# Windowed attention, Fourier mixing and an MLP on one core: new landing times in the planner, a later start for the last batch's loads, and a split last output tile

## The chip, the cores and the metric

One core of a Trainium2 chip. The metric is the device time of one execution in microseconds (us), median of several runs. The kernel before has 281.84 us, the median of five runs (280.18, 281.34, 281.84, 282.03, 282.28).

The engines of the core work side by side, each through its own queue in order: PE (TensorE, matmuls, with the weight loads PEld beside it), DVE (VectorE), ACT (ScalarE), POOL (GpSimd), SP (SyncE, which here only issues transfers). A transfer is issued by an engine's queue and lands later; semaphores tell other engines when.

## The reference

Four batches of 768 rows, 8 heads of 64, so rows of 512. First attention, in which a row sees the 96 rows up to itself and the first 8 rows, with a bias that falls with the distance:

```python
scores = scale * q @ k.T + bias
scores = np.where(is_global | is_local, scores, -1e9)
x = softmax(scores) @ v
```

Then the heads are put side by side, and per batch:

```python
mixed = np.real(np.fft.fft(np.fft.fft(x, axis=1), axis=2))
u = x + mixed
un = (u - mean(u)) / np.sqrt(var(u) + 1e-06)
out = u + np.maximum(un @ w_ch1, 0.0) @ w_ch2
```

with w_ch1 of 512 x 2048 and w_ch2 of 2048 x 512. Inputs and output are fp32; the matmuls work in fp16.

## The kernel before

**Names.** b is the batch (0 to 3). Within a batch, attention goes by pairs of heads, hp 0 to 3; n = 4b + hp counts pairs over all batches, so q7 and k7 are the q and k of batch 1's last pair, and q12 to q15 belong to batch 3. The MLP goes by chunks of 256 rows, three to a batch: c = 3b + pr, 0 to 11, each with two row tiles t of 128.

**Attention.** `load` (L353) issues q, k (384 KB each) and v (two transfers of 192 KB) of a pair on SP into staging buffers of tag qs (3) and vs (2). `cast_qk` (L400) makes fp16 of q and k, from batch 1 on by an ACT activation of about 0.8 us or on POOL; v is cast on POOL. `trans` (L489) transposes q and k on PE (tile pt, 12 matmuls at L498) and DVE or ACT evacuates it to qkT. `score` (L519) has three groups g for a pair: PE makes sc, ACT takes the exponential into er (L566; numbered so that er_10 is that of pair 5's second group), DVE multiplies it by the bias mask into ex. `v_global` and `glob` (pvg, pgl) do the eight global rows; `av` (L646, tile pav) makes the result, which DVE divides into x.

**Fourier mixing.** `bounce` (L701) writes x to DRAM in two halves and reads it back in another order of rows as xr, in two transfers (L719); from batch 1 on ACT issues all of this. DVE folds x by sums and differences (tags zy, eA, ww), PE multiplies by cosine and sine tables (`y_unit`, tile py), DVE or ACT evacuates it (zy, L896 and L898), `mirror` (L911) copies four pieces in reverse order on ACT or POOL (L929), and `u_unit` (L952) makes tile pu on PE (16 matmuls, L963), to which DVE adds xr, with the row sums (u, L984). un is the centred u (L1004, L1006); `nt_unit` (L1025) transposes it (ptu, evacuated to unT); squares on ACT (L1013) and two small POOL operations (L1020, L1021) give rstd.

**MLP.** `ph_unit` (L1056): 8 matmuls of 128 x 256 into a bank ph, then a relu into hT on ACT (L1072) or DVE (L1073). `pg_unit` (L1079): a row tile of 128 x 512 in four quarters of 4 matmuls each (L1089); after the last quarter DVE adds rstd * pg + u into ob (L1100) and the tile is stored as 256 KB (L1105), from ACT for c under 6, from SP after. The banks ph and pg are two each, the banks xx, for all else, two. w1 and w2 come in quarters of 512 KB, issued by POOL (L1177, L1180).

**What sets the order.** All instructions are written out by a planner (`Plan`, L18). It keeps a clock for each engine and for the transfers, and for each result a time at which it is expected (`tok`). `run` chooses the PE group that can start first out of four streams: MIX (Fourier mixing), ATT (attention, both with a look ahead of ten), PH and PG (in order); `emit` puts the work that follows a PE group on the engine that would finish it first. The instructions of an engine run in the order in which the planner wrote them, whether its times come true or not; an instruction that waits holds up all behind it on its engine.

For the loads of batches 1 and 2 the planner doesn't compute when they land but takes it from a table, `LAND` (L343), by n and (q, k, v), through `landed` (L346):

```python
pl.tok[key] = max(pl.t["SP"] + 3.0, LAND[n][w])
```

So the table decides where casts of q and k stand on ACT and POOL, when the planner believes a pair can be transposed, what it puts on PE before that, and, through the buffers that come free, in which order SP issues the loads. A load of batch 1 is not written before the bounce of batch 0 has been issued. For batch 2 there is a gate on the chip (L358): `hold` (L1188) issues on SP a transfer of 32 elements from a piece of w2 to DRAM, and that waits until this piece of w2 has been loaded; everything that stands behind it on SP waits with it. Batch 3's loads have no such gate: they are issued when a staging buffer is free.

Of the kernel before, what the change touches and what calls it, by code (L numbers as in the profile page):

```python
# [10 lines left out]
FP32 = mybir.dt.float32  # L11
AF = mybir.ActivationFunctionType
ALU = mybir.AluOpType
# [4 lines left out]
class Plan:  # L18
# [96 lines left out]
    def run(self, streams):  # L115

        left = [list(s) for s, _ in streams]
        while True:
            best = None
            for i, s in enumerate(left):  # L120
                for k, (needs, ring, _) in enumerate(s[:self.LOOK if streams[i][1] else 1]):
                    if not self.known(needs):
                        continue
                    r = self.at(needs, "PE")
                    if ring is not None:

                        there = [(self.rings[g][0], g) for g in ring if self.rings[g]]
                        if not there:
                            continue
                        t, g = min(there)  # L130
                        r = max(r, t + self.SEM)
                    else:
                        g = None
                    c = (max(r, self.t["PE"]), i, k, g or "")
                    if best is None or c < best:
                        best = c
            op = self.first()
            if op is not None and (best is None or op[0] <= best[0]):
                self.emit(op[4])
            elif best is not None:  # L140
                if self.fill is not None and best[0] - self.t["PE"] > 0.6:
                    self.fill(best[0])
                needs, ring, fn = left[best[1]].pop(best[2])
                if ring is not None:
                    self.slot(best[3])
                fn(best[0], best[3])
                self.promote()
            elif not any(left) and not self.pending:
                return
            else:  # L150
                raise RuntimeError("stuck: " + str([[n for n in s[0][0] if n not in self.tok] for s in left if s])
                                   + str([[n for n in p[2] if n not in self.tok] for p in self.pending][:5]))


def mm_us(n, k=1):
    return k * max(n / 2400.0 + 0.0025, 0.029)
# [6 lines left out]
def dve(n):  # L163
    return 0.15 + n / 960.0
# [11 lines left out]
def kernel(  # L176
# [105 lines left out]
    def free(tag, i):  # L282
        i -= NBUF[tag]
        return [("free", tag, i)] if i >= 0 else []

    def buf(tag, i, shape, dtype, users):
        pl.users(("free", tag, i), users)
        return wk.tile(shape, dtype, tag=tag, name=f"{tag}_{i}", bufs=NBUF[tag])
# [24 lines left out]
    def fill(until):  # L313
# [15 lines left out]
        for i in range(n):  # L329
# [10 lines left out]
    TT = {}  # L340


    LAND = {4: (43.5, 43.3, 47.3), 5: (51.6, 55.5, 54.0), 6: (57.4, 60.9, 59.2), 7: (65.9, 67.0, 64.9),  # L343
            8: (79.4, 81.6, 84.8), 9: (86.6, 91.0, 88.2), 10: (92.8, 96.3, 94.8), 11: (100.0, 102.5, 98.4)}

    def landed(n, w):  # L346
        def then(t):
# [5 lines left out]
    def load(b, hp, which):  # L353
        n = HP * b + hp
        h0 = 2 * hp
        vtag, vi = ("u", hp) if b == 0 else ("vs", n - HP)
        stage[("vs", n)] = (vtag, vi)
        gate = [("hold", b)] if b == 2 else [("xri", 0)] if b == 1 else []  # L358
        if which == "v" and b == 0:
            def run():  # L360
                t = buf(vtag, vi, [P, 2 * NS, Dh], FP32, 1)
                stage[("v", n)] = t
                qk_dma(t.rearrange("p (j t) d -> p j (t d)", t=2), v, b, h0)
            pl.later([("SP", 0.45, run)], free(vtag, vi), 0.0, [("ld", "v", n)], dma=1.34)
        elif which == "v":
            def run():
                t = buf(vtag, vi, [P, 2 * NS, Dh], FP32, 1)
                stage[("v", n)] = t
                src = v[b, h0:h0 + 2].rearrange("h s d -> (h s) d").rearrange("(n m t) d -> t m n d", m=64, t=2)
                for t2 in range(2):  # L370
                    nc.sync.dma_start(t[64 * t2:64 * t2 + 64], src[t2])
            pl.later([("SP", 0.9, run)], free(vtag, vi) + gate, 0.0, [("ld", "v", n)], lat=(0.0, 4.0, 6.0, 5.0)[b], dma=2.45, then=landed(n, 2))
        elif b == 0 and hp < 3:
            cell = {}

            def run(cell=cell):
                cell[0] = buf("hT", hp, [P, 2, NS, 2 * Dh], FP32, 2)
                for w, src in enumerate((q, k)):
                    qk_dma(cell[0][:, w], src, b, h0)
            pl.later([("SP", 0.9, run)], free("hT", hp), 0.0, [("ld", "qk", n, w) for w in range(2)], dma=2.68,  # L380
                     then=lambda t: pl.tok.__setitem__(("ld", "qk", n, 0), t - 1.34))
            for w in range(2):
                cast_qk(b, hp, w, lambda w=w, cell=cell: cell[0][:, w], ("hT", hp))
        else:
            for w, src in enumerate((q, k)):
                cell = {}
                i = 2 * (n - 3) + w

                def run(cell=cell, src=src, i=i):
                    cell[0] = buf("qs", i, [P, NS, 2 * Dh], FP32, 1)  # L390
                    qk_dma(cell[0], src, b, h0)
                pl.later([("SP", 0.45, run)], free("qs", i) + gate, 0.0, [("ld", "qk", n, w)],
                         lat=(0.0, 4.0, 6.0, 5.0)[b], dma=1.34, then=landed(n, w))
                cast_qk(b, hp, w, lambda cell=cell: cell[0], ("qs", i))
# [684 lines left out]
    def pg_unit(c, t, part):  # L1079
# [26 lines left out]
            pl.later([("ACT" if c < 6 else "SP", 0.45, st)], [("ob", i)], 0.0, [], [("free", "ob", i)], lat=1.6, dma=0.7)  # L1106
        PG.append((needs, ("pg",) if part == 0 else None, run))


    def dma_const(dst, src, us, tok, needs=()):  # L1110
        pl.later([("SP", 0.45, lambda: nc.sync.dma_start(dst, src.ap()))], needs, 0.0, [tok], lat=0.2, dma=us)

    with tc.manual_schedule():
# [74 lines left out]
        def hold(n, src):  # L1188

            nc.sync.dma_start(dr.tile([1, 32], FP16, tag=f"hold{n}", name=f"hold{n}", bufs=1), src)  # L1190
        pl.later([("SP", 0.5, lambda: hold(2, w2[0:1, 4, 0:32]))], [("w2", 1)], 0.0, [("hold", 2)])
        for b in range(B):
            if b:
                for hp in range(HP):
                    load(b, hp, "qk")
                    load(b, hp, "v")
                    cast_v(b, hp)
            if b == 0:
                for hp in range(HP):
                    trans(b, hp)  # L1200
                    for g in range(3):
                        score(b, hp, g)
                    if hp:
                        v_place(hp - 1)
                v_global(b, (0,))
                glob(b, (0,))
                for jp in range(NP):
                    av(b, (0, 1), jp)
                v_place(3)
                v_global(b, (1,))  # L1210
                glob(b, (1,))
                for jp in range(NP):
                    av(b, (2,), jp)
                for jp in range(NP):
                    av(b, (3,), jp)
            else:
                trans(b, 0)
                trans(b, 1)
                for hp in range(HP):
                    for g in range(3):  # L1220
                        score(b, hp, g)
                    if hp + 2 < HP:
                        trans(b, hp + 2)
                    if hp == 2:
                        v_global(b, (0, 1))
                        glob(b, (0, 1))
                for half in range(2):
                    for jp in range(NP):
                        av(b, (2 * half, 2 * half + 1), jp)
            bounce(b)  # L1230
            fold_d(b, fold_s(b))
            for g in (0, 1, 2, 3):
                if b > 1:
                    y_unit(b, g)
                    continue
                for t in range(len(YG[g]) // 2):
                    y_unit(b, g, [t])
                    if (b, g, t) == (0, 2, 0):
                        u_unit(b, 0)
            mirror(b)  # L1240
            if b:
                u_unit(b, 0)
            u_unit(b, 1)
            for rows in ((0,), (1,)) if b < 2 else ((0, 1),):
                nt_unit(b, 0, rows)
            u_unit(b, 2)
            nt_unit(b, 1)
            nt_unit(b, 2)
        for c in range(NP * B):
            for jp in range(NJ // 2):  # L1250
                ph_unit(c, jp)
            for t in range(2):
                for part in range(4):
                    pg_unit(c, t, part)
        pl.run([(MIX, True), (ATT, True), (PH, False), (PG, False)])
# [35 lines left out]
```

## Time and profile before

| | before |
|---|---|
| median of five runs | 281.84 us (280.18 to 282.28) |
| the profiled execution: its own time | 283.76 us |
| its span, from the first to the last instruction | 282.0 us |
| mean granted TensorE clock over it | 0.986 |
| PE busy | 265.4 us, 94%, 2505 matmuls |
| DVE busy | 178.0 us, 63%, 356 instructions |
| ACT busy | 151.1 us, 54%, 245 |
| POOL busy | 61.1 us, 22%, 118 |
| bytes moved | 38.10 MB, mean 135 GB/s |
| DMA share between 55 and 80 us | 0.9 or more in 39 of 40 slices |

The page of a profile has the busy time of the engines, the span in 40 slices of 7.05 us (a digit is the busy share in tenths; PEclk is the clock that TensorE was granted, in tenths of full speed), the transfers, the chain of work that ended last, and the costliest groups of instructions. L498 is line 498 of the kernel. Beside it there are tables of waits (engine, line, operation, what it waited for), of the chain in order of time, and of stretches chosen by the reader. Issue to landing of the loads is given as lengths of "DMA" pieces in the chain. The largest groups of PE are ph (L1066, 95.7 us) and pg (L1089, 90.9 us), of DVE ex, ob, u and the relus, of ACT er (38.1 us), relus (33.4) and casts of q and k (16.6).

### The profile page before, as it was taken

Reading aid. Unit: us, or ns where it says so; the run is one execution under the profiler, and the core shown is the slowest. Engines: PE = TensorE matmul, PEld = TensorE weight load, DVE = VectorE, ACT = ScalarE, POOL = GpSimd, SP = SyncE. Lnnn points to the kernel's source line nnn. Section 1 sums busy time; section 2 is a strip of 40 time slices with the busy share of each in tenths; the row PEclk is TensorE's granted clock in tenths of the full one; section 3 lists DMA queues with packets and bytes.
Section 4 is the critical chain, followed back from the end, with each engine's and each line's share of the span. In section 5 each row is a group of like instructions: output and inputs, shape, how many; then the busy total and the mean of one; then the engine's idle time right before and its main releaser. Section 6 shows DMA issues by size and latency. Waiting matters only on the chain.

```text
span 282.0 us, 6109 instructions
## 1 busy us (share of the span) xinstructions
PE 265.4 (94%) x2505; PEld 179.3 (64%) x2505; DVE 178.0 (63%) x356; ACT 151.1 (54%) x245; POOL 61.1 (22%) x118
## 2 busy tenths in 40 slices
PE   7688997999599999999999999999999999999994
PEld 3345586887356556686895668665677577757441
DVE  4576936778347999977799565677895535211121
ACT  2877347893472268788537764685057336324000
POOL 1572524264112043361112113011002020100000
PEclk9999999999689999999999999999999999999999
DMA  7999799999987989983046100000540101010111
GB/s 217 291 287 281 171 247 201 194 229 217 245 163 167 299 205 268 242 180 104 1 100 183 74 37 2 38 2 2 148 152 37 41 37 40 0 74 14 63 74 74
DMA packets 63101, 38.10 MB, mean 135 GB/s; under 512 B 20450, under 2 KB 58594, under 8 KB 62946
## 3 DMA queue, kind: packets, MB, share of 16 engines
q1 hardware_dynamic: 51458, 25.66, 37.4%
q10 hardware_dynamic: 7392, 7.87, 9.5%
q0 software_dynamic: 4224, 4.19, 9.1%
q8 instruction: 19, 0.31, 0.5%
q14 instruction: 8, 0.07, 0.1%
HBM read 32.47 MB, written 9.44 MB: 149 GB/s over the span
## 4 chain that ended last, share of the span: by engine, by line
PE 72%; DMA 14%; DVE 5%; SPq 3%; issue 2%; ACT 2%; POOL 1%; ACTq 0%; POOLq 0%
PE pg L1089 28%; PE ph L1066 26%; DMA qs<-in_k_dram 10%; PE sc L543 3%; PE pav L672 3%; PE pt L498 3%; SPq L398 2%; DMA qs<-in_q_dram 2%; PE pu L963 2%; DVE x L692 2%; PE py L879 2%; PE ptu L1035 1%; PE py L882 1%; DMA xd<-x 1%; PE pav L661 1%
## 5 line engine op out<-in xcount | busy, mean ns | idle before, releaser
L1066 PE MATMUL ph<-unT,w 128*128 128x256 f16 x768 | 95.7, 276 | 0.0
L1089 PE MATMUL pg<-w,hT 128*128 128x512 f16 x384 | 90.9, 379 | 0.0
L1066 PEld LDWEIGHTS <-w 128*128 128x128 f16 x768 | 73.0, 99 | 16.5 <-issue 4.4
L1072 ACT ACTIVATE hT<-ph 128x512 f16<-128x512 f32 x56 | 33.4, 597 | 47.9 <-PE ph L1066 47.7
L1089 PEld LDWEIGHTS <-hT 128*128 128x128 f16 x384 | 35.9, 98 | 35.8 <-issue 1.5
L1100 DVE SCALAR_TENSOR_TENSOR ob<-pg,sm,u 128x512 f32<-128x512 f32 x24 | 17.9, 747 | 41.7 <-PE pg L1089 41.6
L566 ACT ACTIVATE er<-sc 128x992 f16<-128x992 f32 (+2 forms) x42 | 38.1, 922 | 8.7 <-PE sc L543 4.8
L1073 DVE TENSOR_SCALAR hT<-ph 128x512 f16<-128x512 f32 x40 | 27.6, 690 | 19.4 <-PE ph L1066 19.1
L581 DVE TENSOR_TENSOR ex<-er,mk 128x992 f16<-128x992 f16 (+2 forms) x42 | 26.8, 650 | 4.2 <-ACT er L566 4.1
L409 ACT ACTIVATE qk<-qs 128x768 f16<-128x768 f32 x20 | 16.6, 840 | 9.8 <-DMA qs<-in_k_dram 7.2
L984 DVE SCALAR_TENSOR_TENSOR u<-pu,xr 128x512 f32<-128x512 f32 x24 | 15.7, 685 | 8.6 <-PE pu L963 7.7
L498 PE MATMUL pt<-ident,qk 128*128 128x128 f16 x192 | 14.1, 225 | 6.0 <-ACT er L566 3.5
L512 POOL COPY kG<-qkT 64x8 f16<-64x8 f16 x32 | 10.6, 330 | 42.3 <-DVE qkT L507 32.0
L692 DVE TENSOR_TENSOR x<-pav,rc 128x512 f16<-128x512 f32 (+1 forms) x27 | 17.1, 632 | 0.9
L498 PEld LDWEIGHTS <-qk 128*128 128x128 f16 x192 | 12.2, 100 | 8.3 <-issue 5.4
L543 PE MATMUL sc<-qkT 64*128 64x256 f16 (+1 forms) x192 | 16.6, 263 | 0.5 <-ACT v L460 0.4
L672 PEld LDWEIGHTS <-ex 128*128 128x128 f16 x352 | 15.0, 97 | 2.5 <-DVE rc L691 0.4
L672 PE MATMUL pav<-v,ex 128*128 128x65 f16 x352 | 16.1, 193 | 0.0
L896 ACT ACTIVATE zy<-py 128x512 f16<-128x512 f32 (+1 forms) x13 | 9.7, 759 | 11.8 <-DVE eA L829 5.2
L1013 ACT ACTIVATE un<-un 128x512 f16<-128x512 f16 x24 | 14.9, 621 | 1.7 <-PE ptu L1035 1.2
L469 POOL CAST v<-vs 128x768 f16<-128x768 f32 x12 | 10.8, 904 | 21.6 <-DMA vs<-in_v_dram 21.5
L507 DVE COPY qkT<-pt 128x1536 f16<-128x1536 f16 x14 | 13.4, 954 | 2.9 <-PE pt L498 2.7
(104 smaller groups left out, 289.0 us busy)
## 6 DMA issues: line engine op xcount, KB each, us to landing
qs<-in_q_dram SPq DMA_DIRECT2D x13, 384.0 KB, 7.0
qs<-in_k_dram SPq DMA_DIRECT2D x13, 384.0 KB, 6.4
vs<-in_v_dram SPq DMA_DIRECT2D x24, 192.0 KB, 7.2
w<-in_moe_w_ch_dram POOLq DMA_DIRECT2D x8, 512.0 KB, 10.1
out_dram<-ob ACTq DMA_DIRECT2D x12, 256.0 KB, 2.1
out_dram<-ob SPq DMA_DIRECT2D x12, 256.0 KB, 2.0
xd<-x ACTq DMA_DIRECT2D x12, 192.0 KB, 3.6
xr<-xd ACTq DMA_DIRECT2D x6, 384.0 KB, 3.8
```

What stands on the lines that cost most here:

```text
L409: A(d, s, AF.Copy)
L498: nc.tensor.transpose(o[:, j % 2], src[:, w, j].rearrange("p h d -> p (h d)"), idn)
L543: nc.tensor.matmul(pa[:, s, c0:c0 + cw], TT[n][lo:lo + 64, 1, i * P:(i + 1) * P], TT[n][lo:lo + 64, 0, i * P:i * P + cw], start=(not inps) ...
L566: A(mine(), cut(pa), AF.Exp, 0.0, 0.125)
L581: VT(o, mine(), m, op=ALU.mult)
L672: nc.tensor.matmul(po[:, jj, hh * 65:(hh + 1) * 65], lhsT, v16[b % 2][:, i, h, 0:65], start=(jp == 0 and a == 0), stop=(a == len(ops) - 1) ...
L692: VT(X[b][:, 2 * jp:2 * jp + 2, first * Dh:(first + nh) * Dh].rearrange("p j (h d) -> p j h d", d=Dh), pv[:, :, :, 0:Dh], rc.to_broadcast( ...
L1066: nc.tensor.matmul(ph[:, a * CH:(a + 1) * CH], w1[:, d, jb * P:(jb + 1) * P], UNT[c][:, d, :], start=(d == 0), stop=(d == ND - 1))
L1072: pl.later([("ACT", act(512), lambda: A(dst, ph, AF.Relu)), ("DVE", dve(512), lambda: V.tensor_scalar_max(dst, ph, 0.0))], [], e, [("h", c ...
L1073: ("DVE", dve(512), lambda: V.tensor_scalar_max(dst, ph, 0.0))],
L1089: nc.tensor.matmul(pg, HT[c][:, jb, t * P:(t + 1) * P], w2[:, jb, :], start=(jb == 0), stop=(jb == NJ - 1))
L1100: V.scalar_tensor_tensor(cell[0], pg, MV[c][:, t, 3:4], UT[c][:, t, :], op0=ALU.mult, op1=ALU.add)
```

## The change

Three edits, all in the parts shown above. The landing times in `LAND` are others: those of batch 1 are mostly earlier, by up to 4.2 us, with q4, k4 and k7 2.2 to 2.7 us later; those of batch 2 are up to 2.4 us earlier, one 0.1 later. The gate of `load` now holds for batch 3 too, by a second small transfer on SP, `hold(3, ...)`, which reads 32 elements of batch 1's xr, of its second half, and so waits until both halves of it have landed. And the last output tile (c = 11, t = 1) is made by a new function, `pg_last`, in two halves of 256 columns: 16 matmuls of 128 x 256 for each, in place of 16 of 128 x 512, an add on DVE and a store of 128 KB on SP for each; its banks may be of tag pg or ph.

```diff
-    LAND = {4: (43.5, 43.3, 47.3), 5: (51.6, 55.5, 54.0), 6: (57.4, 60.9, 59.2), 7: (65.9, 67.0, 64.9),
-            8: (79.4, 81.6, 84.8), 9: (86.6, 91.0, 88.2), 10: (92.8, 96.3, 94.8), 11: (100.0, 102.5, 98.4)}
+    LAND = {4: (46.0, 46.0, 46.5), 5: (50.5, 55.2, 52.3), 6: (53.2, 58.2, 57.1), 7: (62.8, 69.2, 61.8),
+            8: (77.8, 80.0, 83.3), 9: (85.3, 89.0, 87.0), 10: (90.4, 95.5, 93.8), 11: (99.5, 101.5, 98.5)}
...
-        gate = [("hold", b)] if b == 2 else [("xri", 0)] if b == 1 else []
+        gate = [("hold", b)] if b > 1 else [("xri", 0)] if b == 1 else []
...
+    def pg_last(c, t, half):
+
+        b, pr = divmod(c, NP)
+        rs = PAIRS[pr][t]
+        cols = slice(half * 256, half * 256 + 256)
+
+        def run(start, ring):
+            pg = bank(ring, f"pg_{c}_{t}_{half}")
+            for jb in range(NJ):
+                nc.tensor.matmul(pg[:, 0:256], HT[c][:, jb, t * P:(t + 1) * P], w2[:, jb, cols],
+                                 start=(jb == 0), stop=(jb == NJ - 1))
+            e = pl.pe(mm_us(256, NJ), start)
+            i = HP + 2 * c + t + half
+            cell = {}
+
+            def add():
+                cell[0] = buf("ob", i, [P, 256], FP32, 1)
+                V.scalar_tensor_tensor(cell[0], pg[:, 0:256], MV[c][:, t, 3:4], UT[c][:, t, cols],
+                                       op0=ALU.mult, op1=ALU.add)
+            pl.later([("DVE", dve(256), add)], [("rstd", c)] + free("ob", i), e, [("ob", i)], ring=ring, rank=0)
+            pl.later([("SP", 0.45, lambda: nc.sync.dma_start(out[b].rearrange("(m r) d -> m r d", r=6)[:, rs, cols], cell[0]))],
+                     [("ob", i)], 0.0, [], [("free", "ob", i)], lat=1.6, dma=0.4)
+        PG.append(([("h", c, j) for j in range(NJ // 2)], ("pg", "ph"), run))
...
         pl.later([("SP", 0.5, lambda: hold(2, w2[0:1, 4, 0:32]))], [("w2", 1)], 0.0, [("hold", 2)])
+        pl.later([("SP", 0.5, lambda: hold(3, XR[1][0:1, 5, 0:32]))], [("xr", 1)], 0.0, [("hold", 3)])
...
             for t in range(2):
+                if (c, t) == (NP * B - 1, 1):
+                    pg_last(c, t, 0)
+                    pg_last(c, t, 1)
+                    continue
                 for part in range(4):
                     pg_unit(c, t, part)
```

Since the planner writes out everything from its times, the order of the instructions on all engines differs from about 44 us on. On SP, batch 1's loads from the second pair on go q4, k4, v4, q5, v5, q6, k5, v6, k6, t1 (a table), v7, q7, k7 before, and q4, k4, v4, q5, v5, k5, q6, v6, k6, t1, v7, k7, q7 after. On ACT the cast of q6 stands directly behind er_6 after (before: behind the evacuation of unT and er_7), and the cast of k7 is no longer directly ahead of er_12 together with that of q7; that of q7 stands ahead of er_10. On POOL the first two quarters of w2 are issued one behind the other, behind the rstd operations of chunk 1. On PE, pt_4 stands behind pu_2 and part of the first ph groups, and the first quarter of pg_0_0, a score group, pvg_1 and a ph group stand ahead of pt_7.

## Prediction

> **What bounds the kernel now.** I read the slices first: they show where TensorE is not full and where its clock was taken back.
>
> ```profile
> PE   7688997999599999999999999999999999999994
> ...
> PEclk9999999999689999999999999999999999999999
> ```
>
> One slice is 7.05 us. From the twelfth slice (77.6 us) on, every digit of PE but the last is a 9, and over the span PE is busy 265.4 of 282.0 us (94%). A change of order can therefore win only three things: the idle holes of PE before 78 us, the time at a lowered clock (digits 6 and 8 in the second row, 70 to 85 us), and the tail. Every new hole after 78 us is a loss. The waits of PE name the holes:
>
> ```profile
> PE pt L498 <- ACT er L566: 3.5, 1, 3.5
> PE pt L498 <- ACT unT L1045: 1.4, 1, 1.4
> ```
>
> (total, count, longest). Around them the chain of waits, in order of time (start, length, what):
>
> ```profile
> 46.84 0.83 PE pt L498 x12
> ...
> 49.57 7.46 DMA qs<-in_k_dram
> ...
> 59.57 12.53 DMA qs<-in_k_dram
> 72.10 0.02 issue
> ...
> 72.87 0.99 ACT er L566
> 73.86 0.04 issue
> 73.90 1.44 PE pt L498 x12
> 75.34 1.71 PE ph L1066 x8
> ```
>
> The long hole is a late load. The last k of batch 1 (I call it k7: pair 7, counted over all batches) was issued at 59.57 and landed at 72.10; its cast stands ahead of two er activations in ScalarE's queue, and the transposes pt_7 wait for these until 73.90. From landing to PE it took 1.8 us (73.90 - 72.10). The two last rows also show the clock: a group of 12 transposes takes 1.44 us here and 0.67 at full clock (at 107.42), 8 ph matmuls 1.71 against 0.87. The table by stretches (length; busy PE, weight loads, DVE, ACT, POOL; granted clock; DMA share; GB/s) gives its edges, together with the stage in which VectorE is full:
>
> ```profile
> 69.55:72.95 3.40, 0.83 (x8) 0.59 (x7) 0.69 (x1) 0.83 (x2) 0.00 (x0) 1.00 1.22 210
> ...
> 73.00:74.00 1.00, 0.10 (x2) 0.10 (x2) 0.12 (x1) 1.00 (x2) 0.00 (x0) 0.50 1.24 207
> ...
> 79.00:80.00 1.00, 1.00 (x14) 0.59 (x13) 0.66 (x2) 0.30 (x1) 0.00 (x0) 0.61 0.91 136
> ...
> 105.00:120.00 15.00, 14.61 (x144) 9.91 (x144) 14.59 (x35) 12.09 (x19) 5.66 (x10) 1.00 1.08 253
> ```
>
> The clock was 0.50 from 73 to 79.8 us. PE was working from 73.90 to 79.8 of that, so the half clock cost (79.8 - 73.9)/2 = **3.0 us**.
>
> **What the change can win at most, up to 80 us.** Before loses 1.6 (the hole that ends at 46.84: 1.4 named, 1.6 with the hand-over) + 3.7 (the hole before 73.90, likewise) + 3.0 (half clock) = 8.3 us.
>
> **Part 1, the landing times.** They are numbers for the planner alone, but they move instructions on every engine. I stepped through the changed order up to 130 us by hand, each engine in its own order, with the durations of before: 8 ph 0.87, 4 pg 0.86, 12 pt 0.67, 8 ptu 0.45, 4 sc 0.32; on ACT a cast 0.75 from start to start, er 0.88 to 1.0, relu 0.5 to 0.6; on DVE relu 0.6 to 0.69, u add 0.61 to 0.69, the 1024-wide zy 1.23; loads by their issue and landing rows.
>
> - *44 to 50 us.* pt_4 now stands behind other PE work, so the first hole (1.6) closes.
> - *52 to 61 us.* On SP two pairs of neighbours change places: behind v5 it was q6, k5 (issued 46.59 and 49.57) and is k5, q6; the last two were q7, k7 and are k7, q7. What counts is the place in the queue, not the name: the second of each pair lands as the rows of k5 and k7 show. On ACT the cast of q6 now stands early, right behind er_6 (53.8), while q6 lands where k5 did, at 49.57 + 7.46 = 57.0. ACT stands 3.2 us, with the relu of ph_0_4 and er_7 behind it. PE waits: sc_4_1 for er_6 1.4; ph_0_6 1.0 (its bank, a relu on DVE); ph_0_7 1.6 (its bank, the relu of ph_0_4 on ACT); ph_1_0 1.1; pt_6 0.35; pg_0_0 0.35 (w2's first quarter, which POOL issues later, see below). Sum 5.8 us, none longer than 1.6.
> - *The last load.* q7 has k7's old place in SP's queue. ACT comes to its cast at about 67.3; behind the cast stand er_10 and, through it, sc_6_0 on PE, for which there is work up to 70.75 (2.35 us of pg, sc, pvg and ph were moved ahead of it). So a landing up to 70.75 - 1.8 = **69.0** costs nothing, and each us later costs one. Bounds from rows: q7's own old trip (58.05 to 65.4, 7.4 us) from the new issue at 60.1 gives 67.5; k7's trip of 12.5 gives 72.6. I take the nearer row, k7's, because the place and its company are the same: the two first quarters of w2 (512 KB each, issued 59.91 and 61.44 on POOL, landed 68.2 and 71.9). One thing differs: POOL now issues them behind the rstd of chunk 1, at about 61.5, 1.6 us later; with the two queues taking turns, that moves the end forward by half, 0.8. So q7 lands at 72.1 - 0.8 = 71.3, and sc_6_0 waits 71.3 + 1.8 - 70.75 = **2.4 us**.
>
> After up to 80 us: 5.8 + 2.4 = 8.2 lost against 8.3. The old stall is not gone, it is cut into pieces; what falls away is the half clock, if the pieces don't bring it back. **Gain 0.1.**
>
> - *105 to 126 us.* There DVE is busy 14.59 of 15 us and before's chain runs through it (zy, ex, u, unT from 110.72 to 118.33); PE had filler beside it and lost only 0.7. The new order has less: ptu_3_1 waits 1.2 (for the u add of pu_5 on DVE), pt_11 0.55, ph_3_3 0.9 (its relu stands behind the cast of a batch-3 k, which lands later by part 2). 2.6 - 0.7 = **1.9 lost**. At the least nothing, at the most 2.6.
> - *211 to 220 us.* Before, the pg rows stand between the pu groups:
>
> ```profile
> 214.94 0.86 PE pg L1089 x4
> 215.80 0.89 PE pu L963 x16
> ```
>
> After, ACT does two mirror copies (0.52 each) before the evacuation of py_3_1 (1.02), DVE takes that of py_3_2 (1.23), and only one pg quarter (0.86) lies between py_3_2 and the next pu. It waits 0.65 + 0.7 = **1.4 lost**; bounds nothing and 2.3 (both copies and the slower evacuation in full).
>
> **Part 2, the hold.** A 32-element DMA on SP waits until both halves of batch 1's bounced x (xr 1) are there; the row of the like hold for batch 2 is 0.31 us of issue. Behind it on SP stand only batch 3's loads. The last output stores come later on SP, and ACT issues xr itself, so nothing else waits. In before these loads go out from 101.47 on, beside xr (issued 101.99, landed 109.68: 7.3 to 7.7 us; batch 2's xr, alone, took 3.4 to 4.0). So xr 1 may land some 3.5 us sooner, but its first reader, the u add at 113.59, waits for DVE and for PE's pu (to 111.82), not for xr: 3.8 us were spare. Gain nothing. Cost: batch 3's q, k and v start when xr has landed, about 106 instead of 101.5 to 104.6; that is the 0.9 of ph_3_3 above, already counted.
>
> **Part 3, the last tile.** Before the end:
>
> ```profile
> 260.64 17.28 PE pg L1089 x80
> 277.92 0.02 issue
> 277.94 0.75 DVE ob L1100
> ```
>
> then the store, issued at 278.72, landed at 280.76 (2.04). Half an add: the x rows of DVE fall from 0.69 at 512 columns to 0.42 at 256, so 0.27 less. Half a store: 8 packets of 2 KB per DMA engine at 82 ns become 8 of 1 KB, between 0 and 0.33 less; I take 0.25. The first half's add and store lie beside the second half's matmuls (1.7 us). PE: 32 matmuls at 0.1085 (ph rows) = 3.47 against 16 at 0.2157 = 3.45, 0.02 more. **Gain 0.5** (0.25 to 0.6).
>
> **Sum:** -0.1 + 1.9 + 1.4 - 0.5 = **+2.7 us**. On the profiled execution (283.76, span 282.0) that is 286.5; the median of the runs is 281.84, 1.9 below that execution, and the forecast on it is **284.5 us**, slower by 1.0%. All five runs shown are below the profiled one; if some of them had no half clock, its 3.0 is not there to win, which moves the time up.
>
> The Trainium skill speaks to the half clock ("TensorE: Matmul & The Clock Gate", section "Part 1: The HAM clock gate"): PE drops to half after at least one idle window of about 3.4 us, in windows that run freely, and comes back after a busy one. By it none of the new waits (2.4 us at most) fills a window, and the sum stands; the row 69.55 to 72.95 above was not idle but had PE busy for 0.83 of 3.40 us, and the clock dropped all the same, so the measurement says that the rule is too kind, and the drop costs 3.0 more.
>
> **Rivals.**
> 1. *q7 lands by 69.0* (ends not slower). Its place decides nothing if w2's later issue leaves SP's queue alone long enough: for it, q7's old trip of 7.4 us; against it, k7's 12.5 in that place. Then the 2.4 go: +0.3, **282.1**.
> 2. *The half clock comes (or stays).* After's hole of 2.4, with the 0.35 just ahead of it, leaves PE at 0.65 of 3.4 us (19%) from 69.7 to 73.1, less than the 0.83 (24%) that sufficed; it depends on where the edges of the stretches fall. +3.0: **287.5**. Or the pieces at 52 to 61 bring it: there PE is busy 26 to 47% of 3.4 us, by the edges; two such stretches of half clock with PE waiting a third of them anyway cost 2.0, with q7 on time +2.3: **284.1**.
> 3. *The late holes don't open.* The 1.9 and the 1.4 are differences of sub-microsecond waits, 40 to 140 us after the point where I start; if DVE or ACT is a little earlier, they close: 2.7 - 3.3 = -0.6, **281.2**; with q7 also on time -3.0, **278.8**.
> 4. That the edit doesn't do what it says: the hold does hold and the tile is split, by the order of instructions; no chance given.
>
> **How the numbers follow.** Forecast 0.34 (own range 283.2 to 285.5), rival 1 0.24, rival 2 0.20, rival 3 0.22. About 0.5% (1.4 us) is what a measurement of this kernel tells from no change. Faster: 0.12 of rival 3 and 0.04 of rival 1, 0.16. Same: 0.20 of rival 1, 0.10 of rival 3, 0.03 of the forecast, 0.33. Slower: 0.31 and 0.20, 0.51. The range leaves out the ends of rival 3 (0.10) and of rival 2 (0.07): 279.5 to 287.0.
>
> **What would show it.** Right: PE waits of 1 to 1.6 us between 52 and 61 behind ACT's cast of q6 (57.0); a wait of 2 to 3 us at sc_6_0 behind er_10, with q7 landing after 70; PEclk nines throughout; waits of DVE and ACT at 117 to 126 and at pu near 218; xr 1 landing in about 4 us with no effect; the last add about 0.48 us, the last store landing 1.7 to 2.0 after its issue. Wrong: q7 landing before 69, a new dip in PEclk, no PE waits after 100, or a wait at a place that I haven't named.

## The result, and the profile after

The changed kernel takes 282.97 us in the median (44 runs) against 281.58 for the kernel before (79 runs, the five of before among them). The ratio is **1.0056**, 95% interval 1.0039 to 1.0074: slower by about 1.6 us. The forecast was 1.0% slower, the direction is right and the size is about double. Executions of either kernel spread over some 4 us; a few disturbed ones above that are left out of all ratios, means and counts here.

The profiled executions would say the opposite: the span after is 281.5 us, before 282.0. So the trace of after is not read for its length here, but for what stands where. The slices of after, from its page:

```profile
PE   8788999769999999899999999999999999999995
...
PEclk9999999979999999999999999999999999999999
```

The 5 of PE at 70 us is gone, and with it the dip of the clock there. In its place stand 7, 6 at 49 to 63 us, and in the second of these slices a dip of the clock to 7. The waits of PE in after (line that waits, what it waited for, total, times, longest):

```profile
PE ph L1066 <- DVE hT L1073: 2.3, 2, 1.5
...
PE ph L1066 <- ACT hT L1072: 1.2, 1, 1.2
...
PE ptu L1035 <- DVE u L984: 1.0, 1, 1.0
...
PE pu L963 <- ACT zy L896: 0.6, 1, 0.6
...
PE sc L543 <- ACT er L566: 0.5, 1, 0.5
...
PE pu L963 <- DVE zy L898: 0.5, 1, 0.5
```

One wait of 3.5 us has become a row of waits of 0.5 to 1.5. Where the early ones come from stands in ACT's own queue in after (start, length, engine and line, operation, and in brackets the idle time before it and what ended it):

```profile
51.77 0.97 ACT L566 ACTIVATE er<-sc 128x992 f16<-128x992 f32 x1
55.78 0.84 ACT L409 ACTIVATE qk<-qs 128x768 f16<-128x768 f32 x1 [3.03 <-DMA qs<-in_q_dram]
56.53 0.58 ACT L1072 ACTIVATE hT<-ph 128x512 f16<-128x512 f32 x1
57.01 0.96 ACT L566 ACTIVATE er<-sc 128x960 f16<-128x960 f32 x1
```

ACT stands 3.03 us before the cast of q6, with a relu and er_7 behind it, which were ready. The stretches of after (length; busy PE, PEld, DVE, ACT, POOL; granted clock; DMA share; GB/s):

```profile
50.00:55.00 5.00, 3.73 (x36) 2.66 (x34) 2.85 (x4) 2.34 (x4) 1.08 (x3) 1.00 1.12 223
55.00:60.00 5.00, 2.34 (x21) 1.66 (x21) 2.00 (x3) 4.22 (x7) 1.35 (x3) 0.99 1.22 234
60.00:63.30 3.30, 3.30 (x16) 2.25 (x16) 1.17 (x2) 2.87 (x7) 1.89 (x3) 0.50 1.24 230
...
105.00:120.00 15.00, 13.62 (x138) 9.18 (x136) 13.44 (x32) 12.54 (x19) 3.77 (x8) 1.00 1.16 237
211.00:220.00 9.00, 7.98 (x62) 5.12 (x60) 4.53 (x9) 4.29 (x7) 0.86 (x3) 1.00 0.15 58
```

PE lacks 1.3 + 2.7 us between 50 and 60, then works 3.3 us at half clock (1.65 lost), lacks 1.4 between 105 and 120 (before 0.4, its row stands in the prediction) and 1.0 between 211 and 220. Before has no gap in that last stretch:

```profile
211.00:220.00 9.00, 9.00 (x97) 7.19 (x95) 4.31 (x9) 5.52 (x8) 1.47 (x4) 1.00 0.07 29
```

The end of the chain in after:

```profile
260.85 13.81 PE pg L1089 x64
274.66 3.51 PE pg L1118 x32
278.17 0.03 issue
278.19 0.48 DVE ob L1126
```

The add is 0.48 in place of 0.75; the last store was issued at 278.70 and landed at 280.40, 1.70 us in place of 2.04. From the start of the last add to the landing it is 2.21 us against 2.82, less 0.06 for the 32 smaller matmuls: the tail wins 0.55 us.

### The profile page after: what moved, and what is told of

Read it like the earlier page. It is cut to its first block, busy times and chain, and to the rows that moved or that the text cites. A ratio compares the mean times of both kernels' runs of the same rounds, so it can differ in the third digit from the quotient of the medians.

```text
span 281.5 us, 6139 instructions
## 1 busy us (share of the span) xinstructions
PE 265.2 (94%) x2521; PEld 180.3 (64%) x2521; DVE 181.3 (64%) x358; ACT 152.0 (54%) x248; POOL 58.1 (21%) x114
## 4 chain that ended last, share of the span: by engine, by line
PE 78%; DVE 9%; DMA 5%; SPq 2%; ACT 2%; POOL 1%; issue 1%; DVEq 0%; ACTq 0%; POOLq 0%
PE ph L1066 29%; PE pg L1089 27%; DMA qs<-in_q_dram 5%; PE sc L543 4%; PE pav L672 3%; PE pu L963 3%; PE pt L498 3%; DVE u L984 2%; PE py L875 2%; SPq L398 2%; PE py L879 2%; DVE x L692 2%; PE ptu L1035 1%; PE pg L1118 1%; PE py L882 1%
## 5 line engine op out<-in xcount | busy, mean ns | idle before, releaser
L1089 PE MATMUL pg<-w,hT 128*128 128x512 f16 x368 | 87.8, 379 | 0.0
L1072 ACT ACTIVATE hT<-ph 128x512 f16<-128x512 f32 x58 | 34.5, 597 | 51.3 <-PE ph L1066 51.3
L1089 PEld LDWEIGHTS <-hT 128*128 128x128 f16 x368 | 34.5, 98 | 33.2 <-issue 1.1
L1100 DVE SCALAR_TENSOR_TENSOR ob<-pg,sm,u 128x512 f32<-128x512 f32 x23 | 17.2, 749 | 37.5 <-PE pg L1089 36.8
L1073 DVE TENSOR_SCALAR hT<-ph 128x512 f16<-128x512 f32 x38 | 26.1, 689 | 16.8 <-PE ph L1066 16.6
L581 DVE TENSOR_TENSOR ex<-er,mk 128x992 f16<-128x992 f16 (+2 forms) x42 | 27.6, 665 | 8.1 <-ACT er L566 8.0
L409 ACT ACTIVATE qk<-qs 128x768 f16<-128x768 f32 x21 | 17.3, 839 | 11.3 <-DMA qs<-in_q_dram 4.4
L512 POOL COPY kG<-qkT 64x8 f16<-64x8 f16 x32 | 9.6, 301 | 51.2 <-DVE qkT L507 38.8
L330 PE MATMUL fill<-eg 128*128 128x512 f16 x45 | 12.7, 433 | 1.4 <-DVE eg L1151 1.2
```

What stands on the lines that cost most here:

```text
L409: A(d, s, AF.Copy)
L581: VT(o, mine(), m, op=ALU.mult)
L1072: pl.later([("ACT", act(512), lambda: A(dst, ph, AF.Relu)), ("DVE", dve(512), lambda: V.tensor_scalar_max(dst, ph, 0.0))], [], e, [("h", c ...
L1073: ("DVE", dve(512), lambda: V.tensor_scalar_max(dst, ph, 0.0))],
L1089: nc.tensor.matmul(pg, HT[c][:, jb, t * P:(t + 1) * P], w2[:, jb, :], start=(jb == 0), stop=(jb == NJ - 1))
```

## Experiments

The theory, with the result known, was that the order which the new landing times make gives back early, in small waits, what it saves at pt_7, and that late waits come on top. Its rivals, numbered anew for this section: rival 1 was the hold, rival 2 the clock. Twelve kernels ran, four at a time on one chip, each with 12 runs (`w2late` and `fx4` 6), beside 23 to 35 runs of the kernel before. PE's waits below are the gaps of over 0.1 us between its matmuls, summed in the one profiled execution of each.

| kernel | ratio to before | 95% interval | PE waits after 43 us | of these after 90 us |
|---|---|---|---|---|
| before, on record | 1 | | 5.3 | 0.3 |
| after, on record | 1.0056 | 1.0039 to 1.0074 | 6.5 | 2.4 |
| `again` (before) | 1.0003 | 0.9961 to 1.0045 | 2.6 | 0.3 |
| `tail` | 0.9999 | 0.9962 to 1.0037 | 5.4 | 0.5 |
| `land` | 1.0022 | 0.9980 to 1.0063 | 4.7 | 1.1 |
| `hold` | 1.0030 | 0.9986 to 1.0074 | 5.8 | 1.1 |
| `after2` | 1.0054 | 1.0019 to 1.0090 | 6.5 | 3.1 |
| `nohold` | 0.9975 | 0.9942 to 1.0008 | 3.8 | 1.2 |
| `freehold` | 1.0039 | 1.0005 to 1.0073 | 6.6 | 2.8 |
| `warm` | 1.0032 | 1.0000 to 1.0065 | 5.7 | 2.6 |
| `physhold` | 0.9945 | 0.9908 to 0.9982 | 3.8 | 0.7 |
| `w2late` | 0.9898 | 0.9842 to 0.9954 | 2.1 | 1.0 |
| `fx4` | 1.0275 | 1.0221 to 1.0329 | 11.4 | 5.1 |
| `w2late_tail` | 0.9930 | 0.9894 to 0.9966 | 6.8 | 5.1 |

### Each part alone: `tail`, `land`, `hold`, and before again

```diff
 tail:  + pg_last and its call, nothing else of the change
 land:  + the new LAND, nothing else
 hold:
-        gate = [("hold", b)] if b == 2 else [("xri", 0)] if b == 1 else []
+        gate = [("hold", b)] if b > 1 else [("xri", 0)] if b == 1 else []
+        pl.later([("SP", 0.5, lambda: hold(3, XR[1][0:1, 5, 0:32]))], [("xr", 1)], 0.0, [("hold", 3)])
 again: the kernel before
```

> The kernel before with the split last tile alone. Theory (early waits of PE behind a cast of q6 on ACT, the clock drop that they bring, and small late waits eat what the new order saves; the tail by itself wins): -0.5 us, 0.998 of before, the last add 0.48 us and the last store landing 1.7 to 2.0 us after its issue. Rival 1 (the hold costs, by batch 3's later loads) and rival 2 (the clock alone: before seldom drops it, after often) say the same of this run; if it isn't faster the loss of the change must be larger than thought.

> The kernel before with the new landing times alone. Theory: all of the loss is here, so +1.5 to +2.5 us (1.005 to 1.009), with PE waits of 0.5 to 1.5 us at 52 to 60 us behind the cast of q6, and no wait of over 1 us before pt_7. Rival 1 (the hold): within 0.5 us of before. Rival 2 (clock): slower by 0.5 to 1.5 with a lower mean granted clock than before's in its runs, and equal to before among runs at full clock.

> The kernel before with the hold of batch 3's loads alone. Theory: 0 to +0.6 us, xr of batch 1 lands in about 4 us in place of 7.3 and its first reader comes no earlier. Rival 1: +1.5 to +2 us, with waits of PE behind casts or transposes of batch 3 at 115 to 130. Rival 2: no change.

> The kernel before, unchanged, for the spread: ratio 1.000 within 0.003. The profile on record has a PE wait of 3.5 us before pt_7 and 6.8 us of half clock. Theory: these belong to the order, so they are there again, the wait of 3 to 4 us in every execution, the clock below 0.995 in most. Rival 2: in most executions the clock stays full, and the profile on record is an exception.

None of the four is clear of 1: the parts are smaller than these runs can tell apart. `tail` shows in its profile what after shows (add 0.48, store 1.70). Its runs can't confirm the half microsecond. `land`, at +0.6 us, lies below what the theory said, though its interval (-0.6 to +1.8) touches it; `hold`, at +0.8, lies between the theory and rival 1, and xr's second half took 5.2 us there, not about 4. What the profiles do tell is where the waits belong. `land` has the early waits and no wait of PE before pt_7; `hold` has the old wait, and a new late one:

```profile
PE pt L498 <- ACT er L566: 3.4, 1, 3.4
...
PE pu L963 <- DVE unT L1047: 1.1, 1, 1.1
```

Neither has a wait at 211 to 220: PE is busy 9.00 of 9.00 us there in both. Between 105 and 120 PE lacks 0.9 us in `land` and 1.1 in `hold`, against 0.4 in before and 1.4 in after. So of the late waits a part at 105 to 120 comes with either edit, and those at 211 to 220 come only when both are there; the prediction had put all of them under the landing times.

`again` answers the question on before: of four profiled executions of before's early order (before, `again`, `tail`, `hold`) three have the 3.4 to 3.5 us before pt_7. In `again` the clock had fallen earlier (its dip is in the eighth slice, 48.7 to 55.6 us, behind a wait of 2.0 before pt_4), PE came to pt_7 later, k7 landed earlier (at 70.8 in place of 72.1), and only 0.27 was left. Over the three sets, 58 of 81 executions of before ran at a mean granted clock of 0.991 to 0.997, 18 at 0.998 or more; the profile on record, with 0.986 and 6.8 us of half clock, had about twice the usual share. That fits its own time, 2.2 us above the median, and is likely a part of why after's profile looks faster than before's.

### With and without the hold, and its wait without its order: `after2`, `nohold`, `freehold`, `physhold`

```diff
 after2: the changed kernel
 nohold: the changed kernel without these two
-        gate = [("hold", b)] if b > 1 else ...
-        pl.later([("SP", 0.5, lambda: hold(3, XR[1][0:1, 5, 0:32]))], [("xr", 1)], ...)
 freehold: the changed kernel with
-        hold(3, XR[1][0:1, 5, 0:32])
+        hold(3, w2[0:1, 4, 0:32])
 physhold: nohold, and in the run() of batch 3's first load, ahead of its dma_start
+        hold(3, XR[1][0:1, 5, 0:32])
```

> The changed kernel again, on the chip of the three runs beside it. Both theories: 1.003 to 1.008 of before. The waits of PE at 52 to 60 us (0.5 to 1.5 each) come again, since the order makes them; the drop of the clock at about 60 us comes in some executions only.

> The changed kernel without the hold (new landing times and split last tile). Alone, the hold gave 1.003 and the landing times 1.002, both within their uncertainty. Theory as it stands now (the late waits of PE near 117 and 218 us come with the hold, the early ones with the landing times): the late waits go, the early ones stay, 0.7 to 1.2 us faster than the changed kernel, 0.999 to 1.002 of before. Rival (late waits come from the landing times, as the prediction had it): they stay, within 0.5 us of the changed kernel.

> The changed kernel with the order of every engine as it is, but the second small transfer reads a piece of w2 that has long landed, so that it waits for nothing: batch 3's loads go out as soon as their buffers are free. Theory A (the wait on the chip costs: loads of batch 3 land late): 0.7 to 1.2 us faster than the changed kernel, the waits near 117 us shorter. Theory B (the planner's other order costs, not the wait): the waits near 117 and 218 us stay as they are, within 0.4 us of the changed kernel, while xr of batch 1 takes 7 us again.

> The kernel with the new landing times and the split tile and no hold in the planner (it gave 0.9975), but with the hold's transfer put ahead of batch 3's first load on SP, at no time of the planner: the chip waits as in the changed kernel, the order of all other instructions is that without the hold. Theory B (the hold costs by the planner's other order, not by its wait): within 0.4 us of the kernel without the hold, so 0.996 to 0.999 of before, xr of batch 1 landing in about 4 us. Theory A (the wait costs): 1.0 us or more slower than that, 1.001 to 1.004, with longer waits of PE at 115 to 126.

`after2` repeats the result. Without the hold the kernel is at 0.9975, with it, on the same chip, at 1.0054: on top of the new landing times the hold costs 0.8% (2.1 us by the means, 280.37 against 282.44; 0.7 to 1.2 were expected). `freehold` and `physhold` take it apart. `freehold` keeps the order that the planner made for the hold (by the traces the engines' instructions are in the same order as after's to the end), but nothing waits on the chip, and batch 3's loads start at 102.0 in place of 104.6. It stays at 1.0039, with the late waits of the changed kernel: its waits of ptu for DVE's u (1.0) and of pu for ACT's and DVE's zy (0.6 and 0.5) are those of after. The xr of batch 1 took 4.4 us by the half whose landing is recorded, not the 7 expected. `physhold` keeps the wait (the small transfer goes out on SP at 103.66, once xr has landed, and batch 3's first load at 104.00) and the order without it: 0.9945. So theory B holds: **what costs is the order that the planner writes for a later start of batch 3's loads, not the later start.** In the queues of PE, DVE and ACT of after (start, length) it looks so at 216 us:

```profile
217.70 0.27 PE L963 MATMUL pu<-t,zy 128*128 128x128 f16 x2 [0.45 <-DVE zy L898]
218.54 0.96 PE L963 MATMUL pu<-t,zy 128*128 128x128 f16 x14 [0.56 <-ACT zy L896]
...
216.42 1.23 DVE L898 CAST zy<-py 128x1024 f16<-128x1024 f32 x1 [3.21 <-PE py L879]
...
216.42 1.15 ACT L929 ACTIVATE ww<-zy 128x512 f16<-128x512 f16 x2 [3.03 <-PE py L879]
217.47 1.01 ACT L896 ACTIVATE zy<-py 128x1024 f16<-128x1024 f32 x1
```

The last py group ends at 216.4, one quarter of pg (0.86 from start to start) follows it, and pu waits for two evacuations of py: DVE's starts at 216.42 and ACT's only at 217.47, behind two mirror copies. Without the hold there is one quarter of pg between as well, and no wait:

```profile
214.60 1.06 PE L963 MATMUL pu<-t,zy 128*128 128x128 f16 x16
...
213.28 1.23 DVE L898 CAST zy<-py 128x1024 f16<-128x1024 f32 x1 [1.93 <-PE py L882]
...
214.52 1.01 ACT L896 ACTIVATE zy<-py 128x1024 f16<-128x1024 f32 x1
```

Here DVE's evacuation starts at 213.28, before the last py group has ended (213.9), and pu runs without waiting for the one on ACT, which ends only at 215.5.

The waits after 90 us fall from 2.4 to 3.1 with the planner's hold to 0.7 to 1.2 without it, by 1.2 to 2.4 us: as much as the hold costs, though only single executions say so. Single executions do differ: up to 109 us the order on PE, DVE, ACT and POOL is the same with the hold and without, yet the early wait ahead of chunk 1's first ph group was 1.3 to 1.5 us in after, `after2`, `freehold` and `land`, and 0.4 and 0.5 in `nohold` and `physhold`. Why the planner makes a worse order from a later time wasn't tried further. Whether the wait by itself wins something (`physhold` against `nohold`: 0.9945 and 0.9975, on two chips) can't be said from these intervals.

### The clock: `warm`

```diff
+            if (n, g) == (4, 2):
+                for _ in range(13):
+                    nc.tensor.matmul(pa[:, 0, 0:256], w1[:, 0, 0:P], w1[:, 0, 0:256], start=True, stop=True)
             for i, c0, cw in tiles:
```

> The changed kernel with 13 more matmuls of 128x256 (1.4 us), whose result nothing uses, ahead of the score group that runs before the last of the early waits (1.5 us before the first ph group of chunk 1). They fill that wait. Theory: the clock drop at about 60 us comes from the row of waits at 52 to 60; with one filled it comes seldom, mean granted clock 0.998 or more in most executions, 0.5 to 1.0 us faster on the mean. Rival: the drop does not depend on this wait; as many executions at 0.994 as without (about half), time within 0.4 us or later by the filling.

The wait of 1.5 us is filled, and the profiled execution has full clock. In 7 of 9 executions the clock was at 0.998 or more, against 23 of 47 in after's two sets, and the mean is 0.3 us below `after2`'s. That leans the way of the theory, but neither number is clear of chance, and the time gained is less than expected. **Rival 2 (the clock alone) falls** on another count: after keeps its clock more often than before does (23 of 47 against 18 of 81), and among the executions at full clock it is still slower, 281.73 (after) and 282.10 (`after2`) against 279.59 to 279.96 for before on the three chips. In after a drop goes with 1.4 us: 283.10 in the mean of 17 executions at 0.991 to 0.997, 281.73 in that of 17 at 0.998 or more.

### Why the last load of batch 1 lands late: `w2late`, `w2late_tail` and `fx4`

In before the last load (k7) was issued at 59.57, 0.34 us ahead of w2's first quarter, and took 12.53 us. In after the last load (now q7) was issued at 58.73, 1.6 us ahead of it, and took 6.67: it landed at 65.40.

```diff
 w2late: before; w2late_tail: tail; each with
+                if i == 4:
+                    nc.gpsimd.memset(w2[:, 0:4, :], 0.0)
                 nc.gpsimd.dma_start(w2[:, 4 * a:4 * a + 4, :],
 fx4: nohold, and in LAND
-            5: (50.5, 55.2, 52.3), 6: (53.2, 58.2, 57.1), 7: (62.8, 69.2, 61.8),
+            5: (51.0, 57.0, 53.0), 6: (54.6, 60.5, 59.0), 7: (65.4, 72.1, 64.5),
```

> The kernel before with about 2 us of POOL work (zeros written to w2's first quarter, which the load then overwrites) ahead of the first load of w2, nothing else moved. It goes out behind the last load of batch 1 (k7, issued at 59.6) in place of beside it. Theory (k7 takes 12.5 us because w2's transfers enter the queues beside it; in the changed kernel the last load was ahead of them by 1.6 us and took 6.7): k7 lands 65 to 68, the wait of 3.5 us before pt_7 falls below 1, and the time by 1 to 2.5 us, 0.991 to 0.997. Rival (its place behind all of batch 1's loads is what makes it late): it lands after 70 still, the wait stays, 1.000.

> The kernel before with the split last tile and the later first load of w2: as the run of that beside it, and 0.3 to 0.5 us faster by the tail, 0.989 to 0.996 of before. If k7 is late all the same: 0.998.

> The kernel with the split tile, no hold, and landing times of batch 1 that fit what landed in the runs: q5, k5, v5 51.0, 57.0, 53.0; q6, k6, v6 54.6, 60.5, 59.0; q7, k7, v7 65.4, 72.1, 64.5; batch 2 as in the changed kernel. ACT's cast of q6 stands behind er_7 and not ahead of it. Theory (the early waits are those of ACT at that cast): the waits of PE at 52 to 60 us are half of those without the hold (2.5 us there), 0.5 to 1.5 us faster than that, 0.993 to 0.997 of before. Rival (the early waits come from DVE's relus and the few banks, whatever ACT does): they stay, 0.996 to 1.000.

In `w2late` the load of k7 and the first one of w2 on SP's and POOL's queues:

```profile
59.59 2.82 SPq L398 DMA_DIRECT2D qs<-in_k_dram  x1
```

```profile
59.85 1.80 POOL L1181 MEMSET w<- 128x2048 f16 x1
61.96 0.82 POOL L1182 DMA_DIRECT2D w<-in_moe_w_ch_dram  x1 [0.30 <-POOL w L1181]
```

k7 keeps its place and its time of issue; w2 now follows 2.4 us behind it, and k7 lands at 66.94, after 7.3 us. The wait before pt_7 falls from 3.5 to

```profile
PE pt L498 <- ACT er L566: 0.4, 1, 0.4
```

the clock is full in all five executions counted, and the kernel is at **0.9898** (278.68 us), the lowest ratio of all. That is one added POOL instruction, and no landing time changed. `w2late_tail`, 0.9930, differs from it by its last tile only; it was expected 0.3 to 0.5 us faster than `w2late` and isn't, but the two intervals overlap, so that the tail loses anything isn't said by them. Its profile shows what can come next once PE is early: 5.1 us of waits after 90 us, behind loads and the bounce of batch 1, where `w2late`'s has 1.0. It is the slowest of its 12 executions (281.64; the others 277.61 to 281.11), so it isn't typical.

`fx4` was meant to mend the cast of q6, and that worked as far as it goes: between 50 and 55 us PE waits no more. But in its new order the last load (q7, issued 59.02) has w2's first quarter 0.46 us behind it (59.48), and again it takes 13.0 us. The chain of waits and the waits of PE:

```profile
59.02 13.01 DMA qs<-in_q_dram
```

```profile
PE ph L1065 <- ACT hT L1071: 6.4, 2, 4.8
```

So a mended early stall came with a loss of 2.75%. The last load is late again, with w2's first quarter 1.1 us nearer to it than in `nohold`, and my expectation had left that out. How much of the loss is that load's isn't shown: PE also waits 5.1 us after 90 us, where `nohold` has 1.2, the clock is at 0.975 to 0.986 in all six executions, and `fx4` was not run with w2 held back.

| the last batch-1 load, in | w2's first quarter behind it by | its trip | SP's queue still had to move, when w2's first packet moved |
|---|---|---|---|
| `again` | -1.4 us (ahead of it) | 9.5 us | 0.5 MB |
| `tail` | 0.1 | 12.7 | 0.5 |
| `hold` | 0.3 | 12.6 | 0.5 |
| before | 0.3 | 12.5 | 0.5 |
| `fx4` | 0.5 | 13.0 | 0.6 |
| after, `after2`, `nohold` | 1.6 | 6.7, 6.3, 6.8 | 0.1, 0.2, 0.1 |
| `land`, `warm`, `physhold` | 1.6 | 6.9, 6.1, 6.2 | 0.2, 0.2, 0.2 |
| `w2late_tail` | 2.0 | 6.8 | 0.1 |
| `w2late` | 2.4 | 7.3 | 0.1 |

Thirteen executions (in that of `freehold`, with 1.6 us, the landing isn't recorded) in two groups: the load lands before w2's first quarter, or within 0.8 us of its second. In `again` the trip is shorter, as the load went out later, behind w2's; it landed at 70.8, nearly as late as in the four below it (71.2 to 72.1). The packets of the two queues say why (q1 is the queue of SP and ACT, q0 that of POOL; packets, MB, share of 16 engines). In before up to w2's first packet, 55 to 62.5 us:

```profile
q1 hardware_dynamic: 3650, 1.60, 121.6%
```

In before from there to k7's landing, 62.5 to 72.1, and in after from w2's first packet to q7's landing, 63.2 to 65.4:

```profile
q0 software_dynamic: 1509, 1.51, 94.1%
q1 hardware_dynamic: 1098, 0.54, 26.3%
...
q0 software_dynamic: 363, 0.37, 101.2%
q1 hardware_dynamic: 249, 0.12, 22.6%
```

Alone, SP's queue moved 1.60 MB in 7.5 us, 213 GB/s. Beside w2 it moved 0.54 MB in 9.6 us, 56 GB/s. So what counts is how much it still has to move when w2 starts: 0.54 MB in before, 0.12 in after. By these two rates the difference of 0.42 MB is worth 7.5 us against 2.0, 5.5 us (an estimate); the trips differ by 5.9. The Trainium skill ("DMA: Bandwidth & Descriptors", section "Queues, rings and completion order") says that each DMA engine takes a packet from each queue in turn. Here the two queues did move side by side, but not evenly: SP's had 1098 packets and a quarter of the bytes, POOL's 1509; whether the profile's packets are those that the page means no run shows.

## Why the prediction was right and where it was wrong

- **Direction and sum.** +2.7 us was forecast, 1.0056 of 281.58 is +1.6. That the direction came out right is in part luck: 2.4 of the 2.7 were the wait for the last load, which did not come, and without it the forecast's own sum is +0.3, no change. The span on which the sum was made moved by -0.5; the profiled execution of before was a bad one. The prediction did say that its own time lay 1.9 above the median and that a half clock which isn't usual is not there to win; it counted that as a risk and not in the sum. With the usual drop in before's order (0.994, as in the profiles of `tail` and `hold`: 0.006 of 280, 1.7 us) in place of 3.0, the gain side is 1.3 less, which would have moved the forecast further up.
- **The early pieces: right.** 5.8 us of waits, none longer than 1.6, behind ACT's cast of q6 and DVE's relus, were forecast; 4.1 came in after (0.5, 0.8, 1.2, 1.5 and 0.2), at those groups but for pg_0_0, which didn't wait, and ACT stood 3.0 us where 3.2 were forecast.
- **The last load: this step failed.** "So q7 lands at 72.1 - 0.8 = 71.3, and sc_6_0 waits 71.3 + 1.8 - 70.75 = 2.4 us": it landed at 65.40, and sc_6_0 did not wait. I took k7's row because the place and the company are the same, and let w2's 1.6 us of delay count by half. It counts several times over: until w2 starts, SP's queue moves at 213 GB/s, beside it at 56, and 1.3 us more of a lead (1.6 in place of 0.3) took 5.9 us off the trip. w2's first quarter close behind costs some 6 us, 1.6 us behind costs almost nothing. The prediction's rival 1, at 0.24, is what happened at this place, by the condition that it named (w2's later issue leaves SP's queue alone long enough).
- **The half clock: the forecast left it out, the prediction's rival 2 had it** in its second form, brought by the pieces at 52 to 61, with 2.0 us. It came at 60 us and cost 1.65 in the profile; about half of the executions have one, and they are slower by 1.4.
- **The late waits: right in place, smaller than forecast, put under one edit alone.** 1.9 and 1.4 were forecast, 1.0 (1.4 against 0.4) and 1.0 came, at ptu_3_1, at pt_11 and at pu near 218 us, there behind the two mirror copies on ACT, as the prediction had stepped them; ph_3_3 didn't wait. (Before's own loss at 105 to 120 is 0.4 by its row, 14.61 of 15, not the 0.7 that the prediction set off.) But they were put under the landing times, and the hold was given "Gain nothing" and the 0.9 of ph_3_3 as its cost. `nohold`, `freehold` and `physhold` show that 1.2 to 2.4 us of late waits come when the hold is added to the new landing times, by the planner's order. With the wait on the chip alone (`physhold`) no cost is seen, so the 0.9 was wrong. xr's earlier landing (its two halves took 7.3 to 7.7 us in before, 3.5 and some 4 in after) is not where the late waits are; whether it wins something isn't shown.
- **The tail: right.** 0.5 forecast, 0.55 in the profile; the store fell by 0.34, just past the upper end of 0 to 0.33.
- **The sum with what was measured.** By the mean granted clock over the executions (0.9945 of 81 of before, 0.9957 of 47 of after) half clock costs 1.5 us in before and 1.2 in after. With the waits of the two profiles, after loses 4.1 + 1.2 = 5.3 early, before 1.4 + 3.5 + 1.5 = 6.4; late waits +2.0; tail -0.55. That makes 5.3 + 2.0 - 0.55 - 6.4 = +0.35, and +1.6 was measured. The missing 1.2 us are not settled. They are missing the same way for `w2late`: waits of 2.1 against 5.3 and a full clock should win 4.7, and 2.9 were measured. Both would fit if before's waits are mostly shorter than in its profile, as the 0.27 of `again` is; how often they are wasn't measured.
- **The rule on the clock.** The prediction weighed the Trainium skill ("TensorE: Matmul & The Clock Gate", section "Part 1: The HAM clock gate": half clock after at least one idle window of some 3.4 us) against the row before 72.95, and called the rule too kind. After bears that out: the drop at 60 us follows 3.4 us in which PE was busy 1.30, with no wait above 1.5 us. Its row:

```profile
56.50:59.90 3.40, 1.30 (x12) 0.89 (x12) 1.90 (x3) 3.40 (x7) 1.25 (x3) 1.00 1.21 261
```

## What to carry to other kernels

Before you re-tune a planner's times around one late transfer, look at what is issued next to it on the other queues: here a delay of 2 us on POOL took 5 us off the load and 1% off the kernel, the largest gain of these runs. A gate has two prices, what waits on the chip and what the planner makes of the later time, and they can be taken apart by keeping the one without the other. And take one profiled execution for places and causes, not for totals: here the two on record had the sign of the change wrong.

## What the runs showed of the hardware

- A 384 KB load issued on SP 0.1 to 0.5 us ahead of a 512 KB load on POOL took 12.5 to 13.0 us; the last load in the same place, 1.6 to 2.4 us ahead, took 6.1 to 7.3. SP's queue moved 213 GB/s before the first packet of POOL's load and 56 GB/s beside it.
- The granted clock fell to 0.5 after 3.4 us in which PE was busy 38% of the time, and stayed there for 3.3 us. I had not expected it with waits of 1.5 us at most.
- Executions of one kernel differ in whether that happens: it was at full clock in 18 of 81 of before, 23 of 47 of after, and 16 of 17 of the two with w2's later load.
